# A fused attention and feed-forward kernel: TensorE's fixed order starts at step 12 in place of 15, its halved runs at step 13 in place of 16

## The chip, the cores and the metric

The kernel runs on one core of a Trainium2 chip. A core has a matrix engine (TensorE, PE in the profile, with PEld for its weight loads), a vector engine (VectorE, DVE), an engine for functions (ScalarE, ACT), a general engine (GpSimd, POOL) and an engine that here only issues transfers (SyncE, SP). Each has its own queue of instructions and works through it in order; semaphores make one engine wait for another. The metric is the time of one execution on the device in microseconds. Three runs of the kernel before took 731.11, 731.14 and 731.46 us, so its median is 731.14 us.

## The reference

Causal attention over a window of 128 positions, with the first 4 positions ("sinks") always visible, then a feed-forward network whose activation is h times erf(softplus(h)). All of it is float32.

```python
# q, k, v: 4 batches x 8 heads x 768 positions x 64
scores = scale * np.matmul(q, k.transpose(0, 1, 3, 2))
keep = is_sink | in_window            # pos < 4, or 0 <= rel < 128
scores = np.where(keep, scores, -1000000000.0)
scores = scores - np.max(scores, axis=-1, keepdims=True)
a = np.exp(scores)
a = a / (np.sum(a, axis=-1, keepdims=True) + 1e-09)
x = np.matmul(a, v)                   # to (3072 tokens, 512)
h = x @ w_in                          # 512 -> 2048
sp = np.maximum(h, 0.0) + np.log1p(np.exp(-np.abs(h)))
g = h * erf(sp)
out = g @ w_out                       # 2048 -> 512
```

## The kernel before

**Work units.** Attention is cut into 48 steps: step s is a group of 256 queries (g = s // 4, twelve groups) and a pair of heads (c = s % 4). Four steps make the 256 x 512 input x of the feed-forward network for one group. The network of a group is sixteen blocks of 128 hidden features, and blocks are handled two at a time: `h_26` is the PSUM tile for blocks 26 and 27, counted over all groups. So while attention works on step s, the network works on blocks of an earlier group, four blocks (two pairs) to a step.

**The network's pair.** `hidden` (line 775) makes a pair with 24 matmuls, written `h<-xh,wt` and `h<-xl,wt`; `act` (line 788) takes six passes of ScalarE (lines 796 to 801; the last three write the tiles `u`) and three scalar_tensor_tensor operations of VectorE into `acc`, of which the first reads the PSUM tile `h` and thereby frees it; a cast on VectorE and a subtraction on GpSimd (line 810) give the two halves of `g`; `project` (line 813) adds the pair to the outputs `o` with 12 matmuls. The pool of the tiles `h` has two buffers (line 145). The weights are split in two parts for this: `whigh` (line 627, `wt<-wf` on ScalarE) and `wlow` (line 632, `wt<-wf,wt` on VectorE), 32 pieces each, the last of them around steps 11 to 13.

**The attention step.** `prep` transposes q and k (`tqk`) and copies them to `kq`; `score` (line 294) makes the scores `ps`; `soft` (line 406) moves the causal corner with predicated copies, takes the scores to `pst` with their maxima on VectorE, and runs four exponentials on ScalarE; `norm` (line 439) scales by the sums; `ptrans` transposes the probabilities (`tp`), copies them (`pt`) and masks them on GpSimd (`uo`, line 487); `strans` transposes the sink columns (`ts`), ScalarE writes them to `sp`, and `sinkw` (line 492) corrects `sp` on VectorE, which also reads `ts` in PSUM; `av` multiplies by v; `xfin` writes the result as `xh` (ScalarE) and `xl` (VectorE).

**Two forms of a step.** For s < NI, `tp`, `ts`, `av` and `tqk` are separate tiles that share a PSUM pool of two buffers, `ps_t` (line 148), in turn. From s = NI on, `together` (line 348) writes one run on TensorE: scores of step s and values of step s - 2 in halves of 64 keys, alternating, then the transposes of step s + 1's k and q and (for s > NI) of step s - 1's probabilities and sinks into one tile `rt`. The value tile `av` then comes from the pool of the tiles `h`, and holds `ts` of step s - 1 as well; `rt` takes the two banks that `ps_t` had. Within the run a no-operation on SyncE (line 386) holds the second half of the values back until the first half is done. The tiles `u` have three buffers, and the results `ot` of the first two groups (line 833) take theirs from the same three; the result's transfer to memory has to land before such a buffer is used again. For s > NI the two casts of the sink values `sv` are made by GpSimd and not by ScalarE (line 285).

**What sets the order.** Every piece of work has a due time in units of one block: step s is at `pos(s)` = 4 s - 6, and the tuples of lines 728 to 742 add offsets to it, one list for s < NF1 and one for the others (there `av`, `score` and `xfin` come just before the unit, the transposes later). Pieces are written in the order of these times, and a scheduler that knows the priorities orders each engine's instructions. On some stretches the order in which pieces are written is imposed on an engine as it stands, by a chain of dependences (class `Line`, line 231). These stretches are set in line 762:

```python
vec.on, ten.on, syn.on, sca.on = a < CEND, a <= last or a > fixed, a < LEAD + 4, a > pos(NI) - 0.295
```

`fixed` is `pos(NF1) - 0.5` (line 724). VectorE's order is imposed up to unit 50, TensorE's at the start and from `fixed` on, ScalarE's from `pos(NI) - 0.295` on.

Of the kernel before, what the change touches and what calls it, by code (L numbers as in the profile page):

```python
# [40 lines left out]

NE, AL = 4, 2
NW = 9
NF1 = 15
NI = 16

PW, EA = 256, 40
O = dict(prep=-100, norm=-100, core=-300, av=-300, load=-400, ptrans=-200, xfin=-100,
# [21 lines left out]
def kernel(  # L70
# [67 lines left out]
    def fast_path():  # L138
        with ExitStack() as st:
# [119 lines left out]
            def prep(s):  # L259

                g, c = divmod(s, NPAIR)
                d = stp[s]
                if s <= NI:
                    tp = ps_t.tile([P, 4, P], F32, tag="t", name=f"tqk_{s}")
# [14 lines left out]
            def sinks(s):  # L279
# [3 lines left out]
                if g % GPB == 0:  # L283
                    for r0 in (0, 32):
                        (nc.gpsimd.tensor_copy if s < NE or s > NI else nc.scalar.copy)(sv[r0 : r0 + 32, c, :], d["sv"])
                    vec.tensor_tensor(sv[64:96, c, :], d["sv"], sv[:32, c, :].bitcast(F32), op=ALU.subtract)
# [7 lines left out]
            def score(s):  # L294
# [32 lines left out]

                if s >= NI:
                    together(s, half)
# [13 lines left out]
            def flip(out, in_, r):  # L343

                x = slice(64 * r, 64 * r + 64)
                ten.transpose(out=out, in_=in_[x], identity=ident[x, x])

            def together(s, half):
# [42 lines left out]
                if s + 1 < NSTEP:  # L391
                    n = stp[s + 1]
                    n["tqk"] = x[:, :4]
                    flips += [t[:, i].rearrange("p h d -> p (h d)") for t in (n["k"], n["q"]) for i in range(2)]
                if NI < s:
                    e["tp"] = x[:, 4:]
                    flips += [(e["pst"][:, i, h, :P]) for h in range(2) for i in range(2)]
                m0 = 8 - len(flips) if s + 1 == NSTEP else 0
                for m, y in enumerate(flips):
                    for r in range(2):  # L400
                        flip(x[:, m0 + m, r, :], y, r)
                if NI < s:
                    e["ts"] = at[:, 1, :P]
# [59 lines left out]
            def ptrans(s):  # L463
# [3 lines left out]
                pt = work.tile([P, 2, 2, P], F32, tag="pt", bufs=1, name=f"pt_{s}")  # L467
                if NI <= s < NSTEP - 1:
                    sca.copy(pt.rearrange("p h i (r t) -> p (h i) r t", r=2), d["tp"])
# [108 lines left out]
            def pos(s):  # L578

                return 3 * s if s < NE else 4 * s - 4 * NE + 3 * NE - 2  # L580
# [142 lines left out]

            fixed = pos(NF1) - 0.5
            for s in range(NE, NSTEP + AL):
                a = pos(s)
                if s < NF1:
                    plan = (
# [4 lines left out]
                else:  # L733
# [5 lines left out]
                        ),  # L739
                        ("q", a - (8.2 if s > NF1 + 1 else 6.5 - 2 * (s - NF1)), s), ("p", a - (4.28 if s > NF1 else 2.87), s),  # L740
                        ("k", a - 2.869, s), ("v", a - 3.839, s),
# [241 lines left out]
```

## Time and profile before

| what | before |
|---|---|
| median of three runs | 731.14 us |
| the profiled execution's own time | 730.77 us |
| its span, first to last instruction | 729.1 us |
| TensorE busy | 695.0 us (95%), mean granted clock 0.994 |
| VectorE busy | 517.6 us (71%) |
| ScalarE busy | 540.8 us (74%) |
| GpSimd busy | 193.4 us (27%) |

The profile is of one execution, whose own time is 1.7 us more than its span and 0.4 us less than the median. Busy time is summed over the span and says little of one stage, since the stages have different limits. TensorE is busy almost without a gap from about 198 us on. Steps 11 to 17 lie between about 140 and 230 us: the scores of step 12 begin at 158.96 us, those of step 13 at 176.49, and the run of step 17 begins at 228.40 us.

### The profile page before, as it was taken

The numbers are of one execution on the slowest core, as the hardware profiler recorded it, in microseconds if no ns is written. First come the engines' busy times: TensorE is split into PE (matmuls) and PEld (weight loads), VectorE is DVE, ScalarE is ACT, GpSimd is POOL, SyncE is SP. The second block draws the span as 40 slices with busy tenths as digits, with TensorE's granted clock in tenths as the row PEclk, the third lists the DMA queues.
The fourth block names the chain that finished last, engine by engine and source line by source line (L and its number), as shares of the span: only waits on it lengthen the run. The fifth ranks groups of instructions, "written<-read, shape, count | busy, mean of one in ns | idle before, by whom it ended". The sixth has DMA issues, their size and how long they took to land. (4 is left out here: it accounts for less than half of the span.)

```text
span 729.1 us, 16134 instructions
## 1 busy us (share of the span) xinstructions
PE 695.0 (95%) x5721; PEld 588.3 (81%) x5721; DVE 517.6 (71%) x1493; ACT 540.8 (74%) x1288; POOL 193.4 (27%) x256
## 2 busy tenths in 40 slices
PE   4798999989999999999999999999999999999996
PEld 2474566777888888988888988988888988988995
DVE  7899998999786666666767667666767667663442
ACT  3576669778788778778878778778878778776663
POOL 2221010333232233234223223234223223232221
PEclk9999999999999999999999999999999999999999
DMA  5778641211212211112212212112212211100000
GB/s 142 213 208 307 212 142 27 63 27 37 60 36 53 59 38 44 55 29 47 58 37 52 59 34 49 55 27 46 59 34 57 58 31 38 41 1 1 30 1 33
DMA packets 100600, 47.40 MB, mean 65 GB/s; under 512 B 89248, under 2 KB 93344, under 8 KB 100512
## 3 DMA queue, kind: packets, MB, share of 16 engines
q1 hardware_dynamic: 99680, 46.16, 22.9%
q8 instruction: 47, 0.77, 0.4%
q14 instruction: 41, 0.34, 0.2%
q10 hardware_dynamic: 832, 0.13, 0.1%
HBM read 37.88 MB, written 6.29 MB: 61 GB/s over the span
## 5 line engine op out<-in xcount | busy, mean ns | idle before, releaser
L241 PE MATMUL o<-wt,g 128*128 128x512 f32 x1056 | 258.1, 393 | 1.1 <-POOLq L951 0.7
L241 PEld LDWEIGHTS o<-wt,g 128*128 128x128 f32 x1056 | 191.7, 188 | 39.3 <-POOLq L951 1.1
L810 POOL TENSOR_TENSOR g<-acc,g 128x512 fp32r<-128x512 f32 x88 | 116.8, 1327 | 382.5 <-DVE g L241 378.9
L241 PE MATMUL h<-xh,wt 128*128 128x256 f32 x1408 | 194.6, 281 | 2.2 <-DVE acc L241 2.1
L241 PEld LDWEIGHTS h<-xh,wt 128*128 128x128 f32 x1408 | 180.0, 189 | 9.0 <-DVE acc L241 3.2
L801 ACT ACTIVATE u<-r 128x512 f32<-128x512 f32 x288 | 162.1, 625 | 5.3 <-DVE gf L241 1.6
L241 DVE SCALAR_TENSOR_TENSOR acc<-u,h 128x512 f32<-128x512 f32 x88 | 60.5, 687 | 135.9 <-PE o L241 79.3
L241 DVE SCALAR_TENSOR_TENSOR acc<-u,acc 128x512 f32<-128x512 f32 x176 | 122.2, 694 | 18.0 <-ACT u L801 0.6
L241 PE MATMUL h<-xl,wt 128*128 128x256 f32 x704 | 110.0, 277 | 0.0
L796 ACT ACTIVATE r<-h 128x512 f32<-128x512 f32 x96 | 57.3, 596 | 68.4 <-PE h L241 68.3
L241 ACT ACTIVATE pst<-pst,kq 128x144 f32<-128x144 f32 x192 | 78.5, 421 | 22.7 <-DVE kq L241 22.4
L241 PEld LDWEIGHTS h<-xl,wt 128*128 128x128 f32 x704 | 93.4, 188 | 0.3 <-DVE wf L241 0.2
L487 POOL TENSOR_SCALAR_AFFINE_SELECT uo<-pt 128x512 f32<-128x512 f32 (+1 forms) x96 | 60.1, 649 | 89.9 <-ACT pt L241 89.8
L241 PE MATMUL ps<-kq 64*64 64x208 f32 (+1 forms) x768 | 70.3, 368 | 7.3 <-ACT kq L241 7.3
L241 PE MATMUL av<-uo,v 64*64 64x192 f32 (+4 forms) x856 | 70.0, 294 | 0.0
L797 ACT ACTIVATE r<-r 128x512 f32<-128x512 f32 x96 | 60.9, 635 | 2.7
L798 ACT ACTIVATE r<-r 128x512 f32<-128x512 f32 x96 | 60.9, 634 | 2.8
L241 PEld LDWEIGHTS ps<-kq 64*64 64x64 f32 x768 | 41.5, 138 | 20.7 <-issue 9.7
L241 PEld LDWEIGHTS av<-uo,v 64*64 64x64 f32 (+1 forms) x856 | 47.7, 134 | 10.3 <-issue 1.9
L241 ACT COPY kq<-rt 128x512 f32<-128x512 f32 (+1 forms) x39 | 19.1, 511 | 46.0 <-PE rt L241 46.0
L241 DVE CUSTOM_DVE_ANT_0 pst<-ps,mask 128x144 f32<-128x144 f32 x192 | 47.6, 304 | 1.6
L241 DVE CAST g<-acc 128x512 fp32r<-128x512 f32 x88 | 38.2, 434 | 8.4
(98 smaller groups left out, 713.7 us busy)
## 6 DMA issues: line engine op xcount, KB each, us to landing
ws<-in_moe_w_in_dram SPq DMA_DIRECT2D x16, 512.0 KB, 5.0
ws<-in_moe_w_out_dram SPq DMA_DIRECT2D x16, 512.0 KB, 7.7
v<-in_v_dram SPq DMA_DIRECT2D x64, 96.0 KB, 2.3
out_dram<-ot SPq DMA_DIRECT2D x24, 256.0 KB, 2.2
q<-in_q_dram SPq DMA_DIRECT2D x95, 64.0 KB, 2.4
k<-in_k_dram SPq DMA_DIRECT2D x95, 64.0 KB, 2.3
v<-in_v_dram SPq DMA_DIRECT2D x32, 64.0 KB, 2.3
kq<-kq SPq DMA_DIRECT2D x32, 64.0 KB, 1.8
```

What stands on the lines that cost most here:

```text
L241: ins = f(*a, **k)
L487: nc.gpsimd.affine_select(out=uo[:, :, i1:, e, :], in_=pt[:, :, i1:, :], pattern=[[0, 2], [0, 2 - i1], [-sg, P]], compare_op=op, fill=0.0, ...
L796: nc.scalar.activation(r, h, AF.Tanh, bias=b_t, scale=0.5)
L797: nc.scalar.activation(r, r, AF.Square, bias=b_v, scale=-0.5)
L798: nc.scalar.activation(r, r, AF.Square, bias=b_r)
L801: nc.scalar.activation(u, r, AF.Square, bias=b_a[i], scale=CS)
L810: nc.gpsimd.tensor_tensor(gl, acc, gh.bitcast(F32), op=ALU.subtract)
```

## The change

Two constants change. TensorE's imposed order, and with it the second list of due times, begins with step 12 and not 15 (`fixed` goes from unit 53.5 to 41.5); the run in halves, the `av` tile in the pool of the `h` tiles, the transposes through `rt`, GpSimd's casts of `sv` and ScalarE's imposed order begin with step 13 and not 16 (for the casts: step 14 and not 17).

```diff
@@ -41,8 +41,8 @@
 
 NE, AL = 4, 2
 NW = 9
-NF1 = 15
-NI = 16
+NF1 = 12
+NI = 13
 
 PW, EA = 256, 40
 O = dict(prep=-100, norm=-100, core=-300, av=-300, load=-400, ptrans=-200, xfin=-100,
```

Up to the transposes of step 11 each engine's order is as before, and from the run of step 17 on TensorE's is again the same. What moves lies between. In the pieces below a name's first number is the step or the block, its last is a running number of the build.

On TensorE, between the transposes of step 11 (`tp_11`) and the blocks 26 and 27, the kernel before has:

```order
L241 MATMUL tp_11_1678<-ident_61,pst_138 128x128
L241 MATMUL ts_11_1687<-ident_61,sh1_140 128x128
L241 MATMUL tp_11_1678<-ident_61,pst_138 128x128 x3
L241 MATMUL h_26_1739<-xh_1_722,wt_8_1341 128x256 x2
L241 MATMUL h_26_1739<-xh_1_722,wt_9_1343 128x256 x2
L241 MATMUL h_26_1739<-xh_1_722,wt_10_1345 128x256 x2
```

and the changed kernel:

```order
L241 MATMUL tp_11_1678<-ident_61,pst_138 128x128 x3
L241 MATMUL av_10_1745<-sp_10_1485,sv_136 128x256
L241 MATMUL av_10_1745<-uo_10_1480,v_10_1158 64x128 x2
L241 MATMUL av_10_1745<-uo_10_1480,v_10_1158 64x256 x2
L241 MATMUL av_10_1745<-uo_10_1480,v_10_1158 64x128 x2
L241 MATMUL ps_12_1753<-kq_134 64x208 x2
L241 MATMUL ps_12_1753<-kq_134 64x224 x2
L241 MATMUL ps_12_1753<-kq_134 64x208 x2
L241 MATMUL ps_12_1753<-kq_134 64x224 x2
L241 MATMUL tqk_13_1775<-ident_61,k_13_1724 128x128 x2
L241 MATMUL tqk_13_1775<-ident_61,q_13_1721 128x128 x2
L241 MATMUL h_26_1788<-xh_1_722,wt_8_1341 128x256 x2
```

The values of step 10, the scores of step 12 and the q and k of step 13 have moved ahead of `h_26`. In the kernel before they stand behind it, and between the scores and `tqk_13` lie the 12 matmuls of an output pair.

The second place is at the transposes of step 12. TensorE before, with the last matmuls of the output pair of blocks 24 and 25 ahead of them:

```order
L241 MATMUL o_1_0_1484<-wt_25_1612,g_25_1735 128x512
L241 MATMUL o_1_1_1485<-wt_25_1612,g_25_1735 128x512
L241 MATMUL tp_12_1875<-ident_61,pst_138 128x128
L241 MATMUL ts_12_1884<-ident_61,sh0_139 128x128
L241 MATMUL tp_12_1875<-ident_61,pst_138 128x128 x3
L241 MATMUL h_30_1936<-xh_1_722,wt_12_1544 128x256 x2
```

TensorE of the changed kernel, with the last matmul of `h_28` ahead of them:

```order
L241 MATMUL h_28_1865<-xl_1_723,wt_15_1556 128x256
L241 MATMUL tp_12_1896<-ident_61,pst_138 128x128 x4
L241 MATMUL ts_12_1905<-ident_61,sh0_139 128x128
L241 MATMUL o_1_0_1490<-wt_24_1558,g_25_1741 128x512
L241 MATMUL o_1_1_1491<-wt_24_1558,g_25_1741 128x512
```

The output pair of blocks 24 and 25 has gone from ahead of the transposes to behind them; the value run of step 11 follows it, and `h_30` only then. On ScalarE the work around the exponentials of step 12 (`pst,kq<-pst,kq`) stands before as:

```order
L801 ACTIVATE u0_27_1846<-r_27_1841 128x512
L801 ACTIVATE u1_27_1849<-r_27_1841 128x512
L801 ACTIVATE u2_27_1852<-r_27_1841 128x512
L241 COPY kq_134<-tqk_13_1824 128x4x128
L241 COPY kq_134<-tqk_13_1824 128x3x16
L241 ACTIVATE pst_138,kq_134<-pst_138,kq_134 128x144 x4
L796 ACTIVATE r_29_1918<-h_28_1859 128x512
```

and in the changed kernel:

```order
L796 ACTIVATE r_27_1847<-h_26_1788 128x512
L241 ACTIVATE pst_138,kq_134<-pst_138,kq_134 128x144 x3
L797 ACTIVATE r_27_1847<-r_27_1847 128x512
L241 ACTIVATE pst_138,kq_134<-pst_138,kq_134 128x144
L630 CAST wt_30_1878<-wf_15_1216 128x512
L798 ACTIVATE r_27_1847<-r_27_1847 128x512
L801 ACTIVATE u0_27_1852<-r_27_1847 128x512
L801 ACTIVATE u1_27_1855<-r_27_1847 128x512
```

The passes for blocks 26 and 27, which were done ahead of the exponentials, now stand around and behind them, and one of them is between the third and the fourth. The third place is on GpSimd around steps 13 to 15. Before, the cast of `sv` is ScalarE's, and GpSimd has only the copy of line 288:

```order
L810 TENSOR_TENSOR g_31_2054<-acc_31_2041,g_31_2054 128x512
L487 AFFINE_SELECT uo_13_2064<-pt_13_2057 128x2x128
L487 AFFINE_SELECT uo_13_2064<-pt_13_2057 128x4x128
L227 MEMSET v_15_2167 32x128
L810 TENSOR_TENSOR g_33_2125<-acc_33_2112,g_33_2125 128x512
L288 COPY sv_136<-sv_136 32x128
```

In the changed kernel it is:

```order
L810 TENSOR_TENSOR g_31_2069<-acc_31_2056,g_31_2069 128x512
L227 MEMSET v_15_2210 32x128
L810 TENSOR_TENSOR g_33_2123<-acc_33_2110,g_33_2123 128x512
L487 AFFINE_SELECT uo_13_2168<-pt_13_2166 128x2x128
L487 AFFINE_SELECT uo_13_2168<-pt_13_2166 128x4x128
L285 CAST sv_136<-v_15_2210 32x128 x2
L288 COPY sv_136<-sv_136 32x128
```

The two masks of step 13 have moved behind the subtraction for blocks 32 and 33, and the two casts for step 15 have come in behind both. VectorE's correction of `sv` for step 15, which reads these casts, stands in its own order between the two predicated copies of step 14; before it stood behind that step's scores. The rest of VectorE's order in this stretch keeps its sequence up to the scores of step 12; behind them `xl` of steps 10 and 11 moves ahead of a weight piece or of the predicated copies, the second weight piece of two moves ahead of `sp` of step 12, and `sp` of steps 13 to 15 moves behind the scores of steps 14 to 16.

## Rows read from the trace of the kernel before

**Rows 1.** Busy time in stretches; after each engine's time its instructions, then clock, DMA

```profile
150.00:165.00 15.00, 13.24 (x96) 10.28 (x95) 13.85 (x34) 11.53 (x29) 4.46 (x6) 1.00 0.08 20
240.00:255.00 15.00, 15.00 (x137) 13.27 (x136) 9.18 (x28) 12.57 (x29) 3.95 (x5) 1.00 0.25 72
```

**Rows 2.** Timeline, TensorE, steps 11 to 13: start, duration, work [idle before, releaser]

```profile
153.60 0.64 PE L241 MATMUL tp<-ident,pst 128*128 128x128 f32 x3
...
157.74 0.28 PE L241 MATMUL av<-sp,sv 128*128 128x256 f32 x1
...
159.88 3.03 PE L241 MATMUL o<-wt,g 128*128 128x512 f32 x12
162.75 0.38 PE L241 MATMUL tqk<-ident,k 128*128 128x128 f32 x2
...
163.67 1.20 PE L241 MATMUL h<-xh,wt 128*128 128x256 f32 x8 [0.33 <-DVE acc L241]
...
170.80 0.30 PE L241 MATMUL tp<-ident,pst 128*128 128x128 f32 x1 [0.80 <-ACT wt L630]
...
172.34 1.21 PE L241 MATMUL h<-xh,wt 128*128 128x256 f32 x8 [0.64 <-DVE acc L241]
```

**Rows 3.** Timeline, VectorE, the same stretch

```profile
156.98 4.61 DVE L241 TENSOR_TENSOR wt<-wf,wt 128x512 fp32r<-128x512 f32 x5
161.60 0.57 DVE L241 TENSOR_TENSOR sp<-ts,sp 32x128 fp32r<-32x128 f32 x2
...
162.93 0.69 DVE L241 SCALAR_TENSOR_TENSOR acc<-u,h 128x512 f32<-128x512 f32 x1
...
166.73 0.89 DVE L241 COPY_PREDICATED ps<-tri,ps 64x256 f32<-64x256 int8 x2
...
168.57 0.69 DVE L241 TENSOR_TENSOR wt<-wf,wt 128x512 fp32r<-128x512 f32 x1
...
169.75 0.17 DVE L241 TENSOR_SCALAR kq<-kq 128x4 f32<-128x4 f32 x1 [0.16 <-ACT pst L241]
...
171.59 0.69 DVE L241 SCALAR_TENSOR_TENSOR acc<-u,h 128x512 f32<-128x512 f32 x1
...
177.05 0.69 DVE L241 SCALAR_TENSOR_TENSOR acc<-u,h 128x512 f32<-128x512 f32 x1
```

**Rows 4.** Timeline, ScalarE, the same stretch

```profile
154.87 0.58 ACT L241 COPY pt<-tp 128x512 f32<-128x512 f32 x1
...
168.00 0.42 ACT L241 ACTIVATE pst<-pst,kq 128x144 f32<-128x144 f32 x1 [1.20 <-DVE kq L241]
...
170.62 0.63 ACT L797 ACTIVATE r<-r 128x512 f32<-128x512 f32 x1
```

**Rows 5.** Timeline, TensorE, the run of step 17 and the next

```profile
228.40 0.28 PE L241 MATMUL av<-sp,sv 128*128 128x256 f32 x1
...
230.80 1.17 PE L241 MATMUL h<-xh,wt 128*128 128x256 f32 x8
...
241.86 0.28 PE L241 MATMUL av<-sp,sv 128*128 128x256 f32 x1
```

**Rows 6.** Timeline, GpSimd: subtraction for g, masks of a step

```profile
157.52 1.72 POOL L810 TENSOR_TENSOR g<-acc,g 128x512 fp32r<-128x512 f32 x1
...
188.16 1.30 POOL L810 TENSOR_TENSOR g<-acc,g 128x512 fp32r<-128x512 f32 x1 [2.42 <-DVE g L241]
189.41 1.02 POOL L487 TENSOR_SCALAR_AFFINE_SELECT uo<-pt 128x256 f32<-128x256 f32 x2
```

**Rows 7.** Groups by shape: the casts of sv on GpSimd; count, busy us, mean ns

```profile
L285 POOL CAST sv<-v 32x128 fp32r<-32x128 f32 x24 | 7.9, 329 | 23.6 <-DMA v<-in_v_dram 22.8
```

**Rows 8.** Transfers of the results: count, size, median us from issue to landing

```profile
out_dram<-ot SPq DMA_DIRECT2D x24, 256.0 KB, 2.2
```

**Rows 9.** Timeline, TensorE, the longest wait of the early stretch

```profile
37.21 1.60 PE L241 MATMUL ps<-kq 64*64 64x208 f32 x16 [3.04 <-ACT kq L241]
```

**Rows 10.** The stretch of 2 us behind that wait, columns as in rows 1

```profile
38.00:40.00 2.00, 2.00 (x17) 1.10 (x11) 1.56 (x4) 0.39 (x2) 0.00 (x0) 0.50 0.66 175
```

## The prediction

> **What bounds the kernel now.** I read the stretches of time first, then the timelines of TensorE, VectorE and ScalarE around steps 11 to 17, and last the order of the changed kernel. The stretches show two regimes. Late in the kernel TensorE is busy for all of 15 us and VectorE for 9.18. Between 150 and 165 us VectorE is busy for 13.85 and TensorE leaves 1.76 idle [rows 1]: the last weight pieces are split there, five in a row for 4.61 us [rows 3], and VectorE, which takes its work in a fixed order, is the bound. The reader sees TensorE's waits for it: 0.33 and 0.64 us for `acc`, which frees a tile `h`, and 0.80 us ahead of the transposes of step 12 [rows 2]. For those the releaser shown is a ScalarE cast, but the transposes read probabilities that VectorE began to scale at 169.75 us [rows 3], so I take VectorE as the cause. From about 172 us on TensorE works through what has piled up, and is the bound. A piece that moves on TensorE ahead of 172 us therefore gains nothing unless VectorE comes earlier, and a piece that is left undone there is paid later in full.
>
> **The change part by part.** I follow TensorE from the end of `tp_11` at 153.60 + 0.64 = 154.24 us [rows 2] to the run of step 17, which begins at 228.40 us [rows 5]. What lies behind keeps TensorE's order, and TensorE is full there, so a shift at that run is the shift of the end.
>
> *The head of step 12.* `av_10` now follows `tp_11` at once and takes its bank of the two in `ps_t`. That bank is free when ScalarE has copied `pt_11`, at 154.87 + 0.58 = 155.45 us [rows 4]: a wait of 1.2 us. Values and scores took 157.74 to 159.88, 2.14 us [rows 2], so they end at 157.6. `tqk_13` takes the other bank, that of `ts_11`, and VectorE reads `ts_11` last, in `sp_11` at 161.60 + 0.57 = 162.17 us, behind the five weight pieces [rows 3]. VectorE's order up to there is unchanged. Before, `tqk_13` stood behind an output pair and came at 162.75 us [rows 2]; now TensorE waits 4.6 us for it. Its 0.59 us (162.75 to 163.67, less the wait of 0.33 [rows 2]) end at 162.8.
>
> A block pair's hidden or output half takes 2.77 us on average: four of them fill 230.80 to 241.86, 11.06 us [rows 5]. `h_26`, an output pair and `h_28` follow, 8.3 us, to 171.1. Here the kernel before had also done the output pair of blocks 24 and 25.
>
> *The transposes of step 12.* They now stand ahead of that pair and wait for VectorE's scaling. VectorE's scores of step 12 stay at 166.73, and the exponentials at 168.00 [rows 3, 4]. A pass of the network, 0.63 us and with the step to the next some 0.66 [rows 4], has come between the third and the fourth exponential, so the scaling starts 0.66 later than 169.75 [rows 3], at 170.41, and the transposes at 170.80 + 0.66 = 171.46 [rows 2]. So of the 4.6 us lost above nearly all would have been lost here anyway. The transposes with their waits took 170.80 to 171.70 (172.34 less 0.64 [rows 2]), 0.90 us: they end at 172.4.
>
> *`h_30`.* The output pair (2.77) and the run of step 13 follow, which I put at the 2.40 us of step 17's (228.40 to 230.80 [rows 5]). The run's value tile takes a bank of the `h` pool, so `h_30` now has to wait for the bank of `h_28`, one pair later than before: that is `acc_29`, which on VectorE was at 177.05 [rows 3], and is at 177.71 when everything behind the scaling is 0.66 later. From the start of such an `acc` to the matmul that waits for it takes 0.75 us (171.59 to 172.34 [rows 2, 3]). `h_30` begins at 178.46, some 0.9 us after TensorE could. ScalarE's passes for it do not decide: from the fourth exponential to the first `u` for block 29 there are a cast, ten passes and copies of 0.5 to 0.66 us, to about 176.6.
>
> *From there TensorE is full.* Up to the run of step 17 lie eight hidden and eight output pairs and the runs of steps 14, 15 and 16: 4 x 11.06 + 3 x 2.40 = 51.44 us [rows 5], to 229.90. That is 1.5 us behind 228.40.
>
> *One more wait, at `h_36`.* The run of step 14 begins at 178.46 + 11.06 = 189.5 and ends at 191.9; `h_34` and an output pair bring TensorE to 197.5. `h_36` takes the bank of `av_12`, which also holds `ts_13`, read last by VectorE's `sp_13`, behind the scores of step 14. Between that step's predicated copies VectorE now corrects `sv` of step 15, and waits for GpSimd's casts, which stand behind `g_33` and the masks of step 13. VectorE's `acc_31` comes about 2.2 us later than before (0.66 from `acc_29`, 0.66 for a pass between the exponentials of step 13, 0.9 for `xl_11` and a weight piece ahead of the scores); `acc_33` follows at once, and its cast ends at about 193.1. On GpSimd 1.30 for `g_33`, 1.02 for the masks [rows 6] and two casts of 0.33 [rows 7] lead to 196.1; on VectorE about 0.3 for `sv`, half of 0.89 for a predicated copy, 1.0 for four scores (166.73 + 0.89 to 168.57) and 0.57 for `sp` [rows 3], 2.3 in all, to 198.4. That is 0.9 behind 197.5, with some 0.1 to 0.2 of hand-over 1.1. No row of before shows this wait, so I bound it: nothing if the casts come ahead of `g_33`, and 2.5 if GpSimd's operations take the long times that the same work also has (1.72 in place of 1.30 for `g` [rows 6], and as much more for the masks). I take 1.1, by the nearer rows.
>
> *And one at `h_38`.* ScalarE copies the results of group 1 just ahead of the passes `u` of block 35, later than before because the exponentials of step 14 stand ahead. The copies take two of the three `u` buffers until their transfers have landed, 2.2 us [rows 8], so the last `u` of block 35 comes some 2.2 us later than ScalarE could, and `acc_37`, which frees the bank for `h_38`, follows. By the pitches above (0.66 a pass, 0.4 an exponential) that is between 1 us too early and 1 us too late; the bounds are 0 and 1, and I take 0.3.
>
> *What costs nothing.* The casts of `sv` leave ScalarE (0.33 us each on GpSimd [rows 7]), which isn't the bound. SyncE's gate for step 13 stands ahead of the loads of `v_14`, which need the end of `av_11` anyway; q and k are asked for a step ahead. Transposes of q and k as part of the run are in the 2.40.
>
> *Sum.* 1.5 + 1.1 + 0.3 = 2.9 us. The profile's own time becomes 730.77 + 2.9 = 733.7; the median of the runs is 0.37 above that time, so I forecast 734.0 us.
>
> **The rivals.** *No wait behind the transposes.* If `acc_29` comes early enough and the casts too, TensorE runs on from 172.4: nine output and eight hidden halves (17 x 2.77 = 47.1) and four runs (9.6), to 229.0, 0.6 late: 731.7 us. For it: each of these waits is under 1.2 us by my count, and VectorE's weight pieces between `acc_27` and `acc_29` may run faster at another place beside GpSimd. Against it: VectorE's order there is a chain of operations without a gap.
>
> *The clock falls.* TensorE idles 1.2 and 4.6 us with 2.1 us of work between. Early in the kernel it idled 3.04 us ahead of 37.21 [rows 9], and from 38 to 40 us the granted clock was 0.50 [rows 10], the lower of its two levels, 1.2 GHz: a loss of 1.0 us in those two. Most of one such loss disappears in the wait for the transposes of step 12 (0.4) and in the one ahead of `h_30` (0.9). If the clock stays low for longer, or falls again, two to four times that loss is to be paid, 2.0 to 4.0, less 1.3: on average 1.7 more, 735.7 us. The Trainium skill (TensorE: Matmul & The Clock Gate, section on HAM oscillation) says that a TensorE left idle for long between bursts starts the next one at half clock, which speaks against this change; by that rule the fall is to be expected here. The rows of before agree with it at 38 us, at 0.50.
>
> *Faster.* The run does in 2.40 us what the separate tiles did in 2.14 + 0.59 + 0.90 = 3.63, so three steps save up to 3.6 us of TensorE, and the waits of 0.33, 0.80 and 0.64 [rows 2] could go: 5.4 us. One mechanism decides it: the transposes of step 12 stand where they are only by VectorE's stretch from 156.98 to 169.75. TensorE itself could be there at 166.4 (157.6 + 0.59 + 8.3 without the wait for `ts_11`); then the run of step 17 begins at 166.4 + 0.9 + 56.7 = 224.0, and the time is 726.7 us. It breaks even when the transposes start before 170.8, with no later wait. For it: only that much of TensorE's work does go. Against it: VectorE's order ahead of the transposes is the old one, operation for operation, and nothing there is removed.
>
> **How the numbers follow.** My forecast has 0.62 (732.6 to 735.4 by itself), the clock 0.10, no wait 0.22, faster 0.06. A measurement of this kernel tells 0.2% from no change, 1.46 us: 729.7 to 732.6 counts as the same. So faster 0.06, same 0.22, slower 0.72. The range for 8 in 10 takes in no wait from below, with 0.9 for what VectorE may gain, 730.8; from above the upper bound at `h_36` (2.5 in place of 1.1), that at `h_38` and a little of the clock's, 736.4.
>
> **What would show it.** Right: on TensorE a wait of about 4.6 us ahead of the first `tqk` matmul at 162.2 us, the first `tp` of step 12 within 0.3 us of 171.5 with an output pair behind it, a wait for `acc` ahead of the hidden pair that follows the run of step 13, at 178.5, and one for VectorE's `sp` ahead of the second hidden pair behind the run of step 14, with VectorE idle for GpSimd at `sv`; the run of step 17 at 231.3. Wrong: `tp` of step 12 clearly before 170.8 us, which would say that VectorE's order or speed ahead of it did change; or a granted clock under 1 behind 162 us that still delays the transposes by over a microsecond; or waits on other tiles than `h` and `ts`.

## The result and the profile after

The changed kernel takes 735.66 us (median of 6 runs, 735.49 to 736.32) against 731.14 (6 runs, 730.19 to 731.48): a ratio of 1.0064, 95% interval 1.0054 to 1.0074, so it is 4.5 us slower. I had forecast 734.0, with 730.8 to 736.4 as the range. The direction and the kind of cause came out as forecast; the forecast is 1.7 us too low, and one step went another way than I wrote.

One figure is needed for all that follows. How early a profiled execution reaches step 11 differs: its scores began at 141.86 us in the profile of before, at 142.51 in this one, and between 141.32 and 142.38 in the eleven kernels below, though TensorE's order up to there is the same in all; I cannot tell these differences from chance. So I compare the *stretch* from the first score matmul of step 11 to that of step 17, 86.75 us before (141.86 to 228.61). After the change it is 90.90 (142.51 to 233.41), **4.15 us longer**; behind it 0.3 us more are added up to the last step's scores, of which 0.1 is left at the last output pair. (The two profiled executions differ by 4.9 us in span: 0.65, 4.15 and 0.1.) To set a time of the new trace beside a forecast one, take 0.65 from it.

TensorE's timeline, steps 11 to 14 (start, duration, work, idle time before and its releaser), answers to [rows 2]:

```profile
154.24 0.64 PE L241 MATMUL tp<-ident,pst 128*128 128x128 f32 x3
156.14 0.38 PE L241 MATMUL av<-sp,sv 128*128 128x256 f32 x1 [1.26 <-ACT pt L241]
...
158.03 1.77 PE L241 MATMUL ps<-kq 64*64 64x208 f32 x16
162.90 0.44 PE L241 MATMUL tqk<-ident,k 128*128 128x128 f32 x2 [3.10 <-DVE sp L241]
...
163.31 1.77 PE L241 MATMUL h<-xh,wt 128*128 128x256 f32 x8
...
167.75 2.91 PE L241 MATMUL o<-wt,g 128*128 128x512 f32 x12
...
173.25 0.60 PE L241 MATMUL tp<-ident,pst 128*128 128x128 f32 x4
...
179.17 0.34 PE L241 MATMUL rt<-ident,k 64*128 64x64 f32 x4 [0.55 <-ACT wt L630]
179.73 1.21 PE L241 MATMUL h<-xh,wt 128*128 128x256 f32 x8
...
190.96 0.28 PE L241 MATMUL av<-sp,sv 128*128 128x256 f32 x1
...
193.36 1.18 PE L241 MATMUL h<-xh,wt 128*128 128x256 f32 x8
...
200.50 1.17 PE L241 MATMUL h<-xh,wt 128*128 128x256 f32 x8 [1.40 <-DVE sp L241]
```

The reader sees the two new waits at the head of step 12 (1.26 and 3.10 us), transposes of step 12 without a wait, and two waits behind: 0.55 us in the run of step 13, and 1.40 ahead of `h_36`. The hidden pair from 163.31 to 167.75 takes 4.44 us in place of 2.8. Why shows in the stretches (time of each engine with its instructions, then granted clock, DMA share):

```profile
150.00:165.00 15.00, 9.87 (x61) 6.73 (x61) 14.29 (x34) 9.84 (x27) 4.80 (x6) 0.84 0.08 20
...
156.00:160.00 4.00, 3.66 (x29) 1.97 (x29) 3.86 (x5) 2.13 (x5) 3.42 (x4) 0.60 0.12 28
160.00:163.00 3.00, 0.10 (x1) 0.10 (x2) 2.94 (x7) 1.73 (x4) 0.04 (x1) 0.96 0.12 32
163.00:168.00 5.00, 5.00 (x30) 4.96 (x31) 4.24 (x8) 1.21 (x3) 1.15 (x1) 0.66 0.27 59
```

From 150 to 165 us VectorE is busy for 14.29 and TensorE for 9.87, where they were for 13.85 and 13.24 at a clock of 1.00 [rows 1]. The granted clock fell twice, its mean being 0.60 from 156 to 160 and 0.66 from 163 to 168 us; its lower level is 0.50, 1.2 GHz. VectorE's timeline, which answers to [rows 3], is the old one moved:

```profile
158.10 4.16 DVE L241 TENSOR_TENSOR wt<-wf,wt 128x512 fp32r<-128x512 f32 x5
162.27 0.57 DVE L241 TENSOR_TENSOR sp<-ts,sp 32x128 fp32r<-32x128 f32 x2
...
170.94 0.17 DVE L241 TENSOR_SCALAR kq<-kq 128x4 f32<-128x4 f32 x1 [0.68 <-ACT pst L241]
...
172.78 0.69 DVE L241 SCALAR_TENSOR_TENSOR acc<-u,h 128x512 f32<-128x512 f32 x1
...
175.54 2.81 DVE L241 TENSOR_TENSOR wt<-wf,wt 128x512 fp32r<-128x512 f32 x2
178.39 0.57 DVE L241 TENSOR_TENSOR sp<-ts,sp 32x128 fp32r<-32x128 f32 x2
178.99 0.69 DVE L241 SCALAR_TENSOR_TENSOR acc<-u,h 128x512 f32<-128x512 f32 x1
...
197.96 0.28 DVE L241 TENSOR_TENSOR sv<-v,sv 32x128 fp32r<-32x128 f32 x1 [1.72 <-POOL sv L285]
```

The last line is VectorE's wait for `sv` in the middle of step 14's scores, which delays `h_36`. `h_30` at 179.73 begins as the first operation of `acc_29` ends (178.99 + 0.69 = 179.68). For the 0.55 us ahead of `rt` the releaser shown is a ScalarE cast, but `rt` takes the bank that `sp` of step 12 reads, and `sp` ends at 178.96. I take it as the cause: in five kernels below, as here, `rt` starts 0.21 or 0.22 us after that `sp`, also where another releaser is shown (mend_tp). `sp` stands right ahead of `acc_29` on VectorE, so the two hold TensorE up together.

### The profile page after: what moved, and what is told of

Same layout as the page of the kernel before. It is cut to its first block, busy times and chain, and to the rows that moved or that the text cites. A ratio compares the mean times of both kernels' runs of the same rounds, so it can differ in the third digit from the quotient of the medians.

```text
span 734.0 us, 16243 instructions
## 1 busy us (share of the span) xinstructions
PE 695.4 (95%) x5773; PEld 590.4 (80%) x5773; DVE 517.8 (71%) x1493; ACT 539.2 (73%) x1284; POOL 195.6 (27%) x260
## 5 line engine op out<-in xcount | busy, mean ns | idle before, releaser
L241 PE MATMUL ps<-kq 64*64 64x208 f32 (+1 forms) x768 | 73.0, 374 | 7.4 <-ACT kq L241 7.3
L241 PE MATMUL av<-uo,v 64*64 64x192 f32 (+4 forms) x884 | 72.4, 294 | 0.0
L241 PEld LDWEIGHTS ps<-kq 64*64 64x64 f32 x768 | 43.1, 141 | 20.7 <-issue 9.6
L241 PEld LDWEIGHTS av<-uo,v 64*64 64x64 f32 (+1 forms) x884 | 49.6, 135 | 10.2 <-issue 1.7
L241 ACT COPY kq<-rt 128x512 f32<-128x512 f32 (+1 forms) x44 | 21.0, 501 | 48.7 <-PE rt L241 47.9
```

Of the source, the lines that this page charges most:

```text
L241: ins = f(*a, **k)
```

## The experiments

Two theories stand against each other. The first is the prediction's: VectorE's chain of work sets the pace up to about 179 us, and TensorE's idle time only moves. The rival: TensorE's idle time and the half clock behind it are the loss. Each kernel is the changed one but for its edit; ratios are to the kernel before, measured beside it. Expected times are on the scale of 731.14 us for the kernel before; where I set a result against one, I give the ratio times 731.14. The stretch is read from one execution of each kernel. That execution's own time is 2.0 us below the kernel's median in mend_wl and 1.6 us above it in p1617, and within 1.0 us of it in the others. The pieces of diff are shortened, with constants written out.

| kernel | ratio (95% interval) | stretch longer than before by, us |
|---|---|---|
| changed kernel | 1.0064 (1.0054 to 1.0074) | 4.15 |
| fill | 1.0076 (1.0062 to 1.0089) | 6.62 |
| fill2 | 1.0058 (1.0044 to 1.0071) | 3.77 |
| sp_first | 1.0040 (1.0027 to 1.0054) | 3.10 |
| sv_act | 1.0069 (1.0056 to 1.0083) | 4.88 |
| sv_late | 1.0042 (1.0028 to 1.0055) | 3.22 |
| order12 | 1.0042 (1.0029 to 1.0056) | 3.09 |
| p1415 | 1.0037 (1.0023 to 1.0051) | 1.60 |
| p1617 | 1.0038 (1.0024 to 1.0052) | 4.28 |
| mend_wl | 1.0025 (1.0015 to 1.0036) | 1.53 |
| mend_fill | 1.0016 (1.0007 to 1.0025) | 1.30 |
| mend_tp | 1.0059 (1.0046 to 1.0073) | 4.14 |

**Is it the clock? fill and fill2.** Both give TensorE transposes of the identity to do while it waits; nothing reads them.

```diff
 # fill: behind ts_11 (8) and behind the scores of step 12 (21)
+ten.transpose(out=t[:, P * (1 + i % 3) : P * (2 + i % 3)], in_=ident, identity=ident)  # t: tile of ts_11
 # fill2: behind the scores of step 12 (20)
+t = hp[13] = mlp.hid_tile(26)
+ten.transpose(out=t[:, 0, P * (i % 2) : P * (i % 2) + P], in_=ident, identity=ident)
```

> The changed kernel with 29 transposes of the identity more on TensorE, written into the unused part of the bank of ts_11 and never read: 8 behind the transposes of step 11 and 21 behind the scores of step 12, so that TensorE is busy in the waits of 1.26 and 3.10 us and its clock has no reason to fall. First theory (VectorE sets the pace): granted clock 1.00 from 154 to 168 us in place of 0.50 to 0.94, hidden pair and output pair behind tqk take 2.8 us each in place of 4.4 and 2.75, the transposes of step 12 start near 171.2 behind a wait of their own, and of that gain of 2 us only 0.7 is left at the run of step 13, where sp of step 12 is waited for: 735.0 (734.5 to 735.6). Clock theory (the half clock is what the change costs): the gain of 1.9 us stays to the end, 733.8 or less.

fill missed its aim. The 21 transposes write columns of the bank of `ts_11` that VectorE's `sp` does not read, and still began only behind it (`sp` ends at 162.15); then they kept TensorE busy at half clock.

```profile
162.21 4.74 PE L242 MATMUL ts<-ident 128*128 128x128 f32 x21 [4.09 <-DVE sp L242]
167.01 0.69 PE L242 MATMUL tqk<-ident,k 128*128 128x128 f32 x2
...
170.80 2.91 PE L242 MATMUL o<-wt,g 128*128 128x512 f32 x12
```

So it does not decide on the clock, but it is a test of the first theory from the other side. Counted from the scores of step 11, `tqk` came 4.8 us later than in the changed kernel (25.20 against 20.39 us). The hidden pair behind it ran nearly at full clock (167.78 to 170.80, 3.02 us in place of 4.44), so the transposes of step 12 came 3.75 us later; the stretch grew by 2.5. Only 1.3 us of TensorE's delay were hidden behind VectorE. Its ratio is 736.7 us, above both ranges.

> The changed kernel with 20 transposes of the identity more on TensorE behind the scores of step 12, written into the bank that the next hidden pair overwrites, which is free by then: TensorE is busy in the wait of 3.10 us for tqk, which itself stays. (The wait of 1.26 us ahead of av_10 is not filled.) First theory (behind that wait VectorE sets the pace): the granted clock is 1.00 from 162 to 168 us, the hidden pair behind tqk takes 2.9 us and not 4.4, TensorE then waits some 1 us for the transposes of step 12, and 0.7 to 1.0 us of 1.5 are left at the step 17: 734.8 (734.3 to 735.3). Clock theory: the 1.5 us stay to the end, 734.0 or less, and what the head of order loses without it is the waits alone.

```profile
159.79 3.54 PE L242 MATMUL h<-ident 128*128 128x128 f32 x20
163.16 0.38 PE L242 MATMUL tqk<-ident,k 128*128 128x128 f32 x2
163.52 1.18 PE L242 MATMUL h<-xh,wt 128*128 128x256 f32 x8
166.35 2.91 PE L242 MATMUL o<-wt,g 128*128 128x512 f32 x12
...
171.85 0.79 PE L242 MATMUL tp<-ident,pst 128*128 128x128 f32 x4
...
178.72 0.34 PE L242 MATMUL rt<-ident,k 64*128 64x64 f32 x4 [1.29 <-ACT wt L631]
179.28 1.18 PE L242 MATMUL h<-xh,wt 128*128 128x256 f32 x8
```

Here the hidden pair takes 2.83 us (163.52 to 166.35), 1.6 less, and the transposes of step 12 start 1.0 us earlier (step 11 began at 142.13 here, so 0.38 is to be taken off the difference of 1.40). (The other 0.6 are lost ahead of the pair: the transposes outlast the wait, and `tqk` comes later by that.) At `h_30` 0.07 us are left (0.45 less 0.38); the wait in the run grew from 0.55 to 1.29. The first theory had expected 0.7 to 1.0 us of gain to be left, the clock theory 1.5: both too much. The ratio, 735.4 us, cannot be told from the changed kernel's. In this execution of the changed kernel the half clock behind `tqk` is hidden.

It is hidden only just. sv_act and sv_late, further down, do the same work up to the run of step 13, but in their executions the clock fell later, so that `tqk` took longer and the pair 4.92 us. ScalarE's first pass for `h_26`, which now stands ahead of the exponentials of step 12, waits for the end of that pair, and VectorE's scaling waits for the exponentials (1.35 us in sv_late, 0.68 in the changed kernel). Counted from the scores of step 11, `h_30` came 0.55 and 0.65 us later there. So VectorE's chain is not free of TensorE.

**The wait for `tqk`: sp_first.**

```diff
-add(LEAD + NF + use(n) - LO, "l", n)
+add(LEAD + NF + use(n) - (LO - 0.66 if use(n) == 12 else LO), "l", n)
```

> The changed kernel with VectorE's correction sp of step 11 put ahead of the five weight pieces instead of behind them, so that the bank for the tqk tiles of step 13 is free at about 158.7 us and not at 162.9; the same operations otherwise on VectorE and TensorE. First theory (VectorE's chain of work up to acc_29 sets the pace, TensorE's wait only stands at another place): the wait of 3.10 us ahead of tqk goes, TensorE then waits some 2 to 2.5 us ahead of the transposes of step 12, which start near 171.0 (173.25 in the changed kernel), the wait for sp of step 12 inside the run of step 13 grows from 0.55 us to 2 or more, and the time falls by 0.7 us at most: 735.0 (734.6 to 735.5). Rival (TensorE's idle time and the half clock behind it are the loss): the hidden pair starts 3.1 us earlier at full clock and what follows with it, 732.5 or less.

```profile
158.44 0.69 PE L241 MATMUL tqk<-ident,k 128*128 128x128 f32 x2
...
169.77 0.89 PE L241 MATMUL tp<-ident,pst 128*128 128x128 f32 x4 [1.99 <-ACT r L796]
...
176.68 0.34 PE L241 MATMUL rt<-ident,k 64*128 64x64 f32 x4 [1.23 <-ACT wt L630]
177.24 1.19 PE L241 MATMUL h<-xh,wt 128*128 128x256 f32 x8
...
198.26 1.18 PE L241 MATMUL h<-xh,wt 128*128 128x256 f32 x8 [1.80 <-DVE sp L241]
```

The wait of 3.10 us is gone and the hidden pair runs nearly at full clock, over 4 us of TensorE; 1.05 us of them reach step 17. Most of the others came up as 1.99, 1.23 - 0.55 and 1.80 - 1.40. That is the first theory's mechanism, with a gain over its 0.7: the ratio is 734.1 us, below its range and well above the rival's 732.5.

**The wait ahead of `h_36`: sv_act and sv_late.**

```diff
 # sv_act: the casts of sv for steps 14 and 15 on ScalarE
-(nc.gpsimd.tensor_copy if s < NE or s > NI else nc.scalar.copy)
+(nc.gpsimd.tensor_copy if s < NE or s > 15 else nc.scalar.copy)
 # sv_late: VectorE's correction of sv for step 15 behind sp of step 13
+if s == 15:
+    follow(vec.last, ins)  # ins: that correction
```

> The changed kernel with the casts of sv for steps 14 and 15 on ScalarE again, as in the kernel before; GpSimd keeps those of the later steps. First theory (VectorE waits 1.72 us for GpSimd's cast at 196.2 us, and by that TensorE's h_36 waits 1.40 us for sp of step 13): VectorE's wait goes, the wait ahead of h_36 falls under 0.3 us, and the time falls by 1.0 to 1.4 us, to 734.5 (734.2 to 734.8). Rival (ScalarE or VectorE is late for the next pair anyway, so the wait only moves on to h_38): the wait ahead of h_36 goes and one of 0.8 to 1.4 us stands ahead of h_38, 735.4 to 736.0.

```profile
197.58 0.62 ACT L285 CAST sv<-v 32x128 fp32r<-32x128 f32 x2 [2.43 <-DMA v<-in_v_dram]
```

Both theories missed. On ScalarE the cast runs no earlier than on GpSimd (197.65 in the changed kernel), because it waits 2.43 us for the transfer of `v_15`. That goes into the buffer of `v_12`, whose last reader, `av_12`, is part of the run of step 14. GpSimd's `g_33` and masks, which I had taken for the cause, end at the same moment by chance. From the run of step 13 to that of step 17 sv_act takes 56.63 us, the changed kernel 56.65 (176.55 to 233.20): nothing gained.

> The changed kernel with VectorE's correction of sv for step 15 put behind sp of step 13, instead of between the two predicated copies of step 14; the casts stay on GpSimd. First theory (v of step 15 can be loaded only when the run of step 14 has ended, since av_12 in that run is the last reader of its buffer; the transfer and the casts of it reach VectorE at 197.7 us on GpSimd as on ScalarE, and VectorE stood still for it): VectorE's wait of 1.72 us ahead of sp of step 13 goes, the wait of 1.40 us ahead of h_36 goes too, and the time falls by 1.4 to 1.7 us: 734.1 (733.8 to 734.6). Rival (TensorE is held by the next thing anyway, acc or u of the pair behind, with the copies of the results in between): less than 0.5 us is gained, and a wait of about 1 us stands ahead of h_36 or h_38 for acc, 735.3 to 736.0.

```profile
199.38 1.09 PE L241 MATMUL h<-xh,wt 128*128 128x256 f32 x8
```

The wait ahead of `h_36` is gone and none takes its place; the same four steps take 54.88 us, 1.77 less, 1.63 of them between the runs of steps 14 and 15. The ratio, 734.2 us, lies in the first theory's range. So this wait is real loss, from VectorE standing still in the middle of step 14's scores for an operand that is needed three steps later, by `av_15`. (The stretch gained less, 0.93, because in this execution the clock fell later and the hidden pair at 163.39 took 4.92 us.)

**Which half of the change: order12.** `NF1 = 12`, `NI = 16`.

> The fixed order of TensorE from step 12, and the run in halves with ScalarE's fixed order only from step 16, as before: one half of the change. First theory (the new order leaves an output pair behind ahead of VectorE's stretch, and the run gives some of it back): the waits ahead of av_10 (1.3 us) and tqk_13 (3 us) are there as in the changed kernel, steps 13 to 15 do in separate tiles what the runs did in 2.40 us each, 1.2 us more each, less the waits for acc_29 and sp_13 that only the run has (about 2 us): 737.3 (736.3 to 738.3). Rival (the run in halves, with its value tile in the pool of h, is what costs): with no run ahead of step 16 the time is that of the kernel before within 1 us, 730.5 to 732.

The fixed order alone makes the stretch 3.09 us longer, three quarters of the loss there. Its ratio, 734.2 us, lies in neither range. Most of the miss of my 737.3 is one number: separate tiles standing together in the fixed order take 13.95 us a step (step 14 begins at 190.96, step 15 at 204.91), where the run takes 13.48 (219.72 to 233.20); a run saves 0.5 us against them, not 1.2. From step 13 on the run then costs 1.06 us more than it saves. The step that loses is 14, with the wait ahead of `h_36` that order12 does not have: 15.11 us (190.96 to 206.07) against 13.95.

**Where the order begins: p1415 and p1617.** `NF1, NI = 14, 15` and `16, 17`.

> The fixed order from step 14 and the run from step 15 (12 and 13 in the changed kernel, 15 and 16 before): the same change, but two steps later, behind the last clump of weight pieces on VectorE. First theory (the order loses what VectorE is late by where it begins): av_12 directly behind the transposes of step 13 waits 1.2 us for the copy of pt_13, tqk_15 finds its bank free because sp of step 13 is not behind weight pieces, the clock stays at 1.00 or falls for less than 2 us, and the time is 731.8 (731.0 to 732.6). Rival (leaving an output pair behind and waiting for the transposes' banks costs wherever the order begins): 733.5 to 735.5, with a wait of 2 us or more for tqk_15.

```profile
187.07 0.39 PE L241 MATMUL av<-sp,sv 128*128 128x256 f32 x1 [0.74 <-ACT pt L241]
189.11 0.44 PE L241 MATMUL tqk<-ident,k 128*128 128x128 f32 x2
...
204.90 1.20 PE L241 MATMUL h<-xh,wt 128*128 128x256 f32 x8 [1.40 <-DVE acc L241]
```

The rival's wait for `tqk` is not there, and the clock stayed at 1.00. But behind the first run a wait of 1.40 us for `acc` appeared that I had not counted, the one that I had forecast for `h_30` in the changed kernel: the run's value tile takes a bank of `h`, so the next hidden pair needs a newer `acc`. The ratio, 733.9 us, lies in the rival's range, but not by the rival's mechanism.

> The fixed order from step 16 and the run from step 17: one step later than in the kernel before, the other direction. First theory (an early start loses at VectorE, a later one loses only what a run saves against separate tiles, 13.95 us a step with them and 13.5 to 13.7 with the run): 0.3 to 0.5 us slower than the kernel before, a ratio of 1.0005 (0.9998 to 1.0015). Rival (each step without the fixed order saves TensorE waits where the order begins): faster by 0.5 us or more, a ratio of 0.9993 or less.

It is 1.0038, 733.9 us, and neither theory had that. The profiled execution was the slowest of five, 1.6 us above the median, so its stretch of 4.28 us is more than the typical loss. Its `av_14` waits 1.73 us for the copy of `pt_15` at 217.29, and the mean clock is 0.57 from 218 to 222 us. The step at which the order begins is no smooth dial; how the rest of this loss comes about I have not followed.

**What is left when the waits are mended: mend_wl, mend_fill, mend_tp.** mend_wl has both edits, sp_first's and sv_late's, and one weight piece behind `acc_29`.

```diff
 # mend_wl
+add(LEAD + NF + use(n) - (LO - 0.66 if use(n) == 12 else LO - 1.6 if n in (28, 29) else LO), "l", n)
 # mend_fill: mend_wl, and ahead of tp_12, into the tile of ts_12
+for i in range(24): ten.transpose(out=t[:, x : x + P], in_=ident, identity=ident)
 # mend_tp: mend_wl, and the transposes of step 12 behind the output pair
+(nm, a + (y if NI <= s < NSTEP - 1 else z + 0.05 * (s == 12)), s)
```

> The changed kernel with three places of VectorE's order mended at once: sp of step 11 ahead of the five weight pieces, sv of step 15 behind sp of step 13, and one of the two weight pieces between acc_27 and acc_29 put behind acc_29. TensorE's order is that of the changed kernel. First theory (each wait of TensorE is one place in VectorE's order, and what remains is the wait of about 2 us for the scaling of step 12): 734.4 for the first, less 1.5 and 0.8: 732.1 (731.4 to 732.8), with no wait of over 0.6 us on TensorE between 176 and 230 us. Rival (VectorE has no time to give, each wait comes up again at the next pair): 733.5 to 734.5, with a new wait of a microsecond or more ahead of h_30, h_32 or h_34.

```profile
170.26 0.89 PE L241 MATMUL tp<-ident,pst 128*128 128x128 f32 x4 [3.25 <-ACT r L798]
...
171.01 4.60 PE L241 MATMUL o<-wt,g 128*128 128x512 f32 x12
175.45 0.28 PE L241 MATMUL av<-sp,sv 128*128 128x256 f32 x1
...
177.85 1.19 PE L241 MATMUL h<-xh,wt 128*128 128x256 f32 x8
```

Between the first theory's 732.1 and the rival: 734.41 us beside 732.61 for the kernel before in that session, by the ratio 733.0. The trace is of the fastest of eight executions, 732.44 us, the others taking 734.04 to 734.79. In it no wait is shown behind the transposes up to the run of step 17, and the stretch is 1.53 us longer than before. What remains is the wait for the scaling, now 3.25 us, and behind it the output pair at half clock, 171.01 to 175.45, 4.44 us. `acc_29`'s first operation ends at 176.70, 1.15 us ahead of `h_30`, so that much of it is not hidden.

> The kernel with VectorE's order mended at three places, and 24 transposes of the identity more on TensorE ahead of the transposes of step 12, written into the bank that ts_12 uses next: they fill the wait of 3.25 us there, behind which the output pair took 4.44 us at half clock. Here the wait for acc_29 is the only one known behind, and VectorE has its first operation done at 176.7 us, while h_30 came at 177.85. Clock theory (this half clock is paid to the end as far as VectorE allows): the output pair takes 2.8 us, h_30 starts near 176.8, 1.0 us is gained: a ratio to the kernel before of 1.0010 (1.0003 to 1.0017), where the same kernel without the transposes had 1.0025. Rival (the time lost there is hidden behind VectorE as in the changed kernel): h_30 within 0.3 us of 177.85, and a ratio of 1.0020 to 1.0030.

```profile
167.85 2.78 PE L241 MATMUL ts<-ident 128*128 128x128 f32 x24
...
170.93 3.01 PE L241 MATMUL o<-wt,g 128*128 128x512 f32 x12
173.78 0.28 PE L241 MATMUL av<-sp,sv 128*128 128x256 f32 x1
...
176.72 1.19 PE L241 MATMUL h<-xh,wt 128*128 128x256 f32 x8 [0.47 <-DVE acc L241]
...
191.25 1.20 PE L241 MATMUL h<-xh,wt 128*128 128x256 f32 x8 [0.80 <-DVE acc L241]
```

The clock is 1.00 and the pair takes 2.85 us. `h_30` starts at 176.72, as forecast, about 1 us earlier, and waits for VectorE again; another wait for `acc`, 0.80 us, comes up at `h_34`, and of the 1 us 0.2 are left in the stretch. The ratio, 1.0016, lies inside what the clock theory gave, and its interval overlaps mend_wl's, so the time alone does not decide. The start of `h_30` does: there the half clock was paid, as far as VectorE allows.

> The kernel with VectorE's order mended at three places, and on TensorE the transposes of step 12 behind the output pair of blocks 24 and 25 instead of ahead of it. First theory (acc_29 on VectorE sets when h_30 can start, wherever TensorE does that pair): the pair fills the wait of 3.25 us at full clock, the transposes start near 170.5, TensorE then waits in the run of step 13 and ahead of h_30 for some 3 us in all, h_30 starts near 176.8 and the ratio is 1.0010 (1.0003 to 1.0017); if the clock falls in these waits, the hidden pair behind takes 4.4 us and the ratio is 1.0030. Rival (the place of the transposes ahead of the pair is what costs): h_30 starts at 175.5 or earlier and the time is that of the kernel before or less, a ratio of 0.999 to 1.000.

```profile
172.13 0.39 PE L241 MATMUL av<-sp,sv 128*128 128x256 f32 x1 [0.37 <-DVE acc L241]
...
174.93 0.34 PE L241 MATMUL rt<-ident,k 64*128 64x64 f32 x4 [0.62 <-ACT u L803]
...
177.16 2.08 PE L241 MATMUL h<-xh,wt 128*128 128x256 f32 x8 [1.77 <-DVE acc L241]
...
194.50 1.21 PE L241 MATMUL h<-xh,wt 128*128 128x256 f32 x8 [1.36 <-DVE acc L241]
```

The rival is refuted: with the transposes behind the pair TensorE waits three times up to `h_30`, 2.76 us in all, and `h_30` starts at 177.16, not at 175.5. The hidden pair then ran at half clock to 181.45, and waits of 0.53 (at 190.39) and 1.36 us followed. The first theory had the wait for `acc_29` and the start of `h_30`, but its 1.0030 for a falling clock was too little beside 1.0059, since it had not counted the later waits. Doing the pair after the transposes, as the change does, is the better order here. No version beat the kernel before.

## Why the prediction was right, and where not

- **The head of step 12: right.** `av_10` waited 1.26 us (1.2 forecast), and `tqk_13` came at 162.25 on the old scale (162.2 forecast), when VectorE had read `ts_11`. The wait shows only 3.10 us and not 4.6 because values and scores took 3.66 us (156.14 to 159.80) at a lowered clock in place of 2.14.
- **The transposes of step 12: wrong in cause.** I had them at 171.46, held by VectorE; they came at 172.60, without a wait. VectorE's scaling was on time (170.29 against 170.41); TensorE was late, since its hidden pair took 4.44 us. The prediction itself named this as a sign of being wrong: a lowered clock behind 162 us that delays the transposes by more than a microsecond. That the forecast came near all the same is in part luck. fill2 shows that this delay cost next to nothing here, since with the pair at full clock `h_30` gains 0.07 us; but in sv_act and sv_late, where the clock fell later and the pair took 4.92 us, some 0.6 us reached `h_30`.
- **`h_30`: right in cause, 0.62 us too early.** It starts as `acc_29` lets it, at 179.08 and not 178.46; the wait itself stands earlier, in the run, for the `sp` right ahead of `acc_29`. The mis-sized term: the two weight pieces ahead of `acc_29` took 2.81 us beside GpSimd's masks and subtraction (174.90 to 177.81), 1.12 + 1.06 before. In fill, where GpSimd stood idle until 177.77, they took 1.29 (176.84 to 178.13). That mend_wl, where one of them stands behind `acc_29`, has `acc_29` at 176.01 fits.
- **`h_36`: right in place, 1.40 us for 1.1; half right in cause.** VectorE waits at `sv` as I wrote, 1.72 us, and sv_late shows that the wait costs 1.77 us to step 17. But GpSimd is only one of two reasons that are equally late; the other is the load of `v_15`, which the run of step 14 holds back (sv_act). The prediction weighed the loads of `v_14` and dismissed them; the same thought for `v_15` was missing.
- **`h_38`: wrong, and small.** 0.3 us forecast, no wait seen.
- **"TensorE is full" at 11.06 us for two pairs of pairs: a little too fast.** From `h_30` to the run of step 14 it took 11.23 (179.73 to 190.96), from `h_34` to the end of the next output pair 5.74 in place of 5.53; such differences make 0.6 us in all. With 0.62 at `h_30` and 0.3 - 0.3 at the two waits they make up the 1.25 us between my 2.9 and the 4.15 measured in the stretch. The run of step 17 came at 232.55 and not 231.3.
- **The rivals.** The clock rival's time, 735.7, is the one measured, but by coincidence: the clock did fall, to 0.60 and 0.66 in two stretches, and what it took on the hidden pair was hidden, by fill2. The Trainium skill (TensorE: Matmul & The Clock Gate, section on HAM oscillation) says that a TensorE left idle for long between bursts starts the next one at half clock. This trace agrees with 0.66 behind the wait of 3.10 us; the fall to 0.60 came behind only 1.26 us, which is not the long wait that the section tells of. *No wait* is refuted by 0.55 and 1.40 us. *Faster* needed the transposes of step 12 before 170.8, and they came at 172.60; and a run saves 0.5 us a step against the separate tiles of order12, not 1.2.

Open remains what made the clock fall at 156 us in some executions and after 160 in others, what slows p1617, and where the 0.6 us of a slower pace come from.

## What to carry to other kernels

Where a slower engine paces a stretch, a wait that is taken from the fast engine comes up again at the next thing it needs from there: sp_first freed over 4 us of TensorE and kept 1.05. Look for waits inside the pacing engine's own order instead; an operand that is needed three steps later should not stand in the middle of work that is needed now (sv_late, 1.77 us for one moved instruction). And a buffer that is read inside a longer fused run comes free later, so the load behind it, too, is moved by the fusion.

## What the runs showed of the hardware that I had not expected

- The clock fell after waits of quite different length: by 156 us, after 1.26 us idle, in the changed kernel (clock 0.60 from 156 to 160) and in fill2 (0.50), but in sv_late the same 1.25 us left it at 1.00 up to 160 and it fell behind a wait of 4.43 (0.51 from 163 to 168). mend_wl and mend_fill have the same order up to there and the same wait of 1.25 us, and from 155 to 160 the clock was 1.00 in one and 0.66 in the other. On the pair that ran at half clock this cost 1.5 (mend_tp) to 2.1 us (sv_late).
- Behind step 17, where TensorE is never idle and the clock 1.00, the profiled executions of five kernels (sp_first, sv_act, sv_late, fill2, p1415) lose another 1.8 us up to the last step's scores, the changed kernel 0.3, mend_fill none. In the steps concerned each matmul of one hidden and one output pair is a little longer: the same twelve output matmuls take 2.96 us at 292.79 in sv_late and 2.91 at 293.75 in the changed kernel. The cause is open. mend_wl's profiled execution does not have it (0.2) and is 1.6 us faster than any of its other seven, which would fit a loss that comes and goes between executions of one kernel; no second trace shows that. It limits what the times of single kernels can tell, and is why the stretch is given beside each ratio.
